# Second gated product of a retention-and-FFN kernel: from 256-column blocks to 512-column twins in two passes

## The chip, the cores and the metric

The kernel runs on one core of one Trainium2 chip. The metric is the device time of one execution in microseconds. The core's engines are named as the profile names them: PE (TensorE matmul), PEld (TensorE weight load, which overlaps PE), DVE (VectorE), ACT (ScalarE), POOL (GpSimd) and SP (SyncE, whose row issues nearly all DMAs). Each engine has its own row of instructions and takes them in order; semaphores order the engines among each other.

## The reference

```python
def _attn_ref(q, k, v):                  # 8 x 8 heads, 576 tokens, head size 64
    scores = scale * np.matmul(q, k.transpose(0, 1, 3, 2))
    gamma = 1.0 - 2.0 ** (-5.0 - np.arange(H, dtype=np.float32))
    rel = pos[:, None] - pos[None, :]
    Dmat = np.where(rel >= 0, gamma[:, None, None] ** rel[None, :, :], 0.0)
    return np.matmul(scores * Dmat[None, :, :, :], v)

def _moe_ref(x, w_in, w_out):            # x 4608 x 512, w_in 512 x 2048, w_out 2048 x 512
    h = x @ w_in
    g = h * np.cos(h)
    return g @ w_out                     # the second gated product

def _moe2_ref(x, w1, w2, w3, w_out):     # w1, w2, w3 512 x 768, w_out 768 x 512
    h = np.maximum(np.maximum(x @ w1, x @ w2), x @ w3)
    return h @ w_out
```

The three run one after the other on float32 data; the change is in `g @ w_out` of the second.

## The kernel before

Every dense product is done by a seven-product scheme on 2 x 2 blocks (Winograd's form of Strassen). The operands are the products' names: `P_A11`, `P_A12`, `P_A22` and the sums `P_S1` to `P_S4`; both the weights and the data are brought into these seven forms beforehand. Each operand is held as a high part (a cast to the reduced type, on ACT) and a low part (what the cast left, a subtraction on DVE), and each product takes three matmuls per pair of 128 x 128 weights: low weight by high data, high by high, high by low.

The 4608 tokens are 9 blocks of 512 columns (`NBLK`, `NB`). Blocks 1 to 8 also form four twins, `m` = 0 to 3 (`NDUO`): a matmul over a twin takes 256 columns of each of its two blocks, 512 in all. Block 0 stands alone. The order of the program:

1. Retention and the first product's first half, `group_in` (L447) with groups k = 0 and 1 of each block; then groups k = 2 and 3 of each block. The gate `h*cos(h)` (`gate`, L505: two ACT and two DVE instructions of 1024 columns for each half of a group) leaves its result in DRAM tensors `gq[j][k]`.
2. The second gated product, `phase_out` (L907): for each block j and each of the four groups k, seven products, in `OUT_ORDER`. `product_out` (L862) issues 12 matmuls of 256 columns for each. The seven products have a PSUM bank each, which collects the four groups; after the last group `finish_out` (L879) combines the banks, and two DMAs write the block of `x2`. `build_out` (L820) loads a group's four quarters and makes differences, high and low parts some slots ahead.
3. The branches: block 0 in three single groups (`single_group`, matmuls of 256 columns), then the twins (`duo_groups`, `product_duo` L416, matmuls of 512 columns), then the output product (`out_duo`, `group_out`).

The order of the work is written by hand. `tick()` (L153) ends a slot (one product, as a rule); `at(n, fn)` puts work n slots ahead, and `tick` issues what is due. So each engine's row is fixed by the program, and an instruction that waits holds back all that stands behind it in its row. Weights are brought into seven forms in the background: `background` (L235) loads and joins raw 64-bit weights and, for the branches ("b") and the output ("o"), stores the forms in DRAM ("stash"); `take` (L344) loads them; `take_split` (L327) makes the second product's forms ("wo") on chip from a stored joined form: four sums (L203 to L206), casts and subtractions (L213 to L229).

Buffers: 8 of 14 KB per partition for weights (`wpool`), 22 of 4 KB for data (`xpool`), 8 PSUM banks. A tile's buffer is given to a later tile, whose first writer waits for the last reader of the old one.

## Time and profile before

| | |
|---|---|
| median of 3 runs (lowest to highest) | 1441.91 us (1441.09 to 1442.17) |
| the profiled execution | 1442.28 us, span 1440.5 us |
| PE busy | 1413.1 us, 98% of the span, 10492 matmuls |
| DVE busy | 1160.7 us, 81% |
| ACT busy | 778.1 us, 54% |
| DMA | 331.52 MB, 230 GB/s over the span |

The span is from the first to the last instruction; the time of an execution has a little around it. A matmul's busy time overlaps its neighbours', so what a matmul costs is read from how many start in a stretch, not from its own duration. The granted clock tells TensorE's clock as a share of its higher level.

### The profile page before, as it was taken

How to read it: one execution, taken by the hardware profiler on the slowest of the kernel's cores; microseconds unless marked ns; L12 is line 12 of the kernel's file. 1: busy time of each engine (PE TensorE's matmuls, PEld its weight loads, DVE VectorE, ACT ScalarE, POOL GpSimd, SP SyncE). 2: the span in 40 equal slices, each digit the busy share in tenths (PEclk: the TensorE clock that was granted, in tenths of full speed). 3: DMA queues.
4: the chain of work that ended last, by engine and by line, in shares of the span. 5: the costliest groups of instructions: out<-in, count | busy, mean ns of one | idle time of the engine just before them, and what ended most of it. 6: DMA issues, size and time to landing. Idle time of an engine off the chain costs nothing.

```text
span 1440.5 us, 26312 instructions
## 1 busy us (share of the span) xinstructions
PE 1413.1 (98%) x10492; PEld 1299.3 (90%) x10492; DVE 1160.7 (81%) x1649; ACT 778.1 (54%) x1259; POOL 178.1 (12%) x128
## 2 busy tenths in 40 slices
PE   7999999999999998999999999999999999999998
PEld 5899999998999998999999999988888888888887
DVE  7988888779787779999999998668576667868875
ACT  4666666667787776444444443344344434534543
POOL 3343443331022000000000000000000000000000
PEclk9999999999999999999999999999999999999999
DMA  9779989868999985365565567723433294435633
GB/s 359 254 280 321 317 285 342 299 259 298 359 387 351 339 288 170 126 224 199 189 210 195 189 227 289 303 74 125 142 129 125 86 372 176 156 132 167 227 117 117
DMA packets 95034, 331.52 MB, mean 230 GB/s; under 512 B 9408, under 2 KB 17600, under 8 KB 88768
## 3 DMA queue, kind: packets, MB, share of 16 engines
q1 hardware_dynamic: 94912, 329.85, 64.4%
q8 instruction: 82, 1.34, 0.4%
q14 instruction: 40, 0.33, 0.1%
HBM read 197.69 MB, written 132.12 MB: 229 GB/s over the span
## 4 chain that ended last, share of the span: by engine, by line
PE 81%; DVE 3%; DMA 3%; issue 1%; ACT 0%; SPq 0%; DVEq 0%; ACTq 0%
PE wo L870 23%; PE d_e L428 13%; PE d_a L406 11%; PE b_e L428 7%; PE b_a L406 6%; PE d_u L1272 5%; PE a_e L428 3%; PE sums L406 3%; PE b_u L1272 2%; PE d_b L406 2%; PE sc L567 1%; PE po L626 1%; PE a_u L1272 1%; DMA k_z<-x2q 1%; PE state L610 1%; PE po L638 1%
## 5 line engine op out<-in xcount | busy, mean ns | idle before, releaser
L870 PE MATMUL wo<-h_g,w_wo 128*128 128x256 f32 x1728 | 313.3, 283 | 0.0
L870 PEld LDWEIGHTS wo<-h_g,w_wo 128*128 128x128 f32 x1728 | 269.9, 192 | 0.0
L870 PE MATMUL wo<-l_g,w_wo 128*128 128x256 f32 x864 | 245.4, 284 | 4.6 <-DVE l_g L843 4.5
L870 PEld LDWEIGHTS wo<-l_g,w_wo 128*128 128x128 f32 x864 | 166.1, 192 | 5.6 <-DVE l_g L843 5.4
L406 PE MATMUL d_a<-x_x,w_wi 128*128 128x256 f32 x864 | 122.5, 290 | 1.0 <-DVE x_x L383 1.0
L523 DVE SCALAR_TENSOR_TENSOR s_a<-t_a,s_a 128x1024 f32<-128x1024 f32 x72 | 93.6, 1300 | 31.1 <-ACT t_a L520 31.0
L428 PE MATMUL d_e<-h_e,w_b 128*128 128x512 f32 x432 | 115.5, 389 | 0.0
L406 PE MATMUL d_a<-x_y,w_wi 128*128 128x256 f32 x864 | 112.6, 287 | 2.5 <-DMA x_y<-xs 2.1
L406 PEld LDWEIGHTS d_a<-x_x,w_wi 128*128 128x128 f32 x864 | 108.3, 190 | 6.7 <-issue 1.9
L838 ACT CAST h_g<-tb_g 128x1024 fp32r<-128x1024 f32 x36 | 37.8, 1051 | 141.1 <-DVE tb_g L375 141.1
L406 PEld LDWEIGHTS d_a<-x_y,w_wi 128*128 128x128 f32 x864 | 108.9, 196 | 2.9 <-ACT ar_wo L184 2.3
L514 DVE SCALAR_TENSOR_TENSOR t_a<-s_a,t_a 128x1024 f32<-128x1024 f32 x72 | 96.0, 1334 | 18.0 <-ACT t_a L510 17.7
L453 ACT ACTIVATE ext<-d_e 128x512 f32<-128x512 f32 x72 | 43.0, 597 | 116.6 <-PE d_e L428 116.3
L428 PEld LDWEIGHTS d_e<-h_e,w_b 128*128 128x128 f32 x432 | 81.0, 188 | 16.8
L196 POOL TENSOR_TENSOR fa_b<-raw_b 128x512 uint32<-128x512 uint32 x18 | 22.5, 1250 | 537.5 <-DVE raw_b L190 506.8
L520 ACT ACTIVATE t_a<-t_a 128x1024 f32<-128x1024 f32 x72 | 76.0, 1055 | 21.9 <-DVE t_a L514 21.8
L594 ACT COPY u<-state 128x128 f32<-128x128 f32 x128 | 31.4, 264 | 96.6 <-PE state L610 96.2
L510 ACT ACTIVATE t_a<-s_a 128x1024 int32<-128x1024 f32 x72 | 76.1, 1056 | 1.3 <-PE d_a L406 0.4
L457 DVE TENSOR_TENSOR ext<-ext,b_e 128x512 f32<-128x512 f32 x36 | 24.7, 686 | 57.5 <-PE b_e L428 57.5
L428 PE MATMUL d_e<-l_e,w_b 128*128 128x512 f32 x216 | 66.5, 389 | 0.0
L406 PE MATMUL b_a<-x_x,w_wi 128*128 128x256 f32 x432 | 61.1, 289 | 0.6 <-DVE u L576 0.6
L406 PE MATMUL b_a<-x_y,w_wi 128*128 128x256 f32 x432 | 58.0, 283 | 1.7 <-DMA x_y<-xs 1.4
(268 smaller groups left out, 3248.4 us busy)
## 6 DMA issues: line engine op xcount, KB each, us to landing
u<-att SPq DMA_DIRECT2D x36, 1024.0 KB, 7.4
gq<-s_a SPq DMA_DIRECT2D x72, 512.0 KB, 5.4
k_g<-gq SPq DMA_DIRECT2D x72, 512.0 KB, 6.0
xs<-x_x SPq DMA_DIRECT2D x63, 512.0 KB, 5.5
x_y<-xs SPq DMA_DIRECT2D x63, 512.0 KB, 7.3
w_b<-st_b SPq DMA_DIRECT2D x9, 1792.0 KB, 11.3
st_b<-p_b SPq DMA_DIRECT2D x27, 512.0 KB, 5.1
mqp<-ext SPq DMA_DIRECT2D x24, 512.0 KB, 3.1
```

The costliest lines, as they stand in the source:

```text
L406: nc.tensor.matmul(h[:, p * HB : (p + 1) * HB], a, b, start=first and p == 0 and i == 0, stop=i == len(terms) - 1, skip_group_check=True,)
L428: nc.tensor.matmul(dst, a, b, start=first and i == 0, stop=i == len(terms) - 1, skip_group_check=True)
L453: nc.scalar.activation(dst, b[:, :n], AF.Copy, scale=scale)
L457: nc.vector.tensor_tensor(out=dst, in0=dst, in1=b[:, :n], op=ALU.add)
L510: nc.scalar.activation(st["t"], s, AF.Copy, bias=0.25)
L514: nc.vector.scalar_tensor_tensor(out=r, in0=s, scalar=MOST_TURNS, in1=st["t"], op0=ALU.min, op1=ALU.subtract)
L520: nc.scalar.activation(r, r, AF.Sin, scale=TURN, bias=HALF_PI)
L523: nc.vector.scalar_tensor_tensor(out=s, in0=f32(st["t"]), scalar=-1.0, in1=s, op0=ALU.max, op1=ALU.mult)
L594: nc.scalar.copy(um, st)
L838: nc.scalar.copy(h, o[pairs[k][2]])
L870: nc.tensor.matmul(b[:, mt * HB : (mt + 1) * HB], a, v, start=first and mt == 0 and p == 0 and i == 0, stop=last and p == len(ws) - 1 and ...
L1272: nc.tensor.matmul(dst, a, v, start=first and p == 0 and i == 0 and (wide or mt == 0), stop=p == 2 and i == 2, skip_group_check=True,)
```

## The change

The gated product is done in two passes over the tokens. A pass takes two of the four groups (`half` 0: k = 0 and 1, `half` 1: k = 2 and 3) through units: a unit is a twin (`m` = 0 to 3) or the lone block (`None`), in the order 0, None, 1, 2, 3 and then None, 0, 1, 2, 3 (`wo_order`). In a twin's unit each matmul has 512 columns, 256 of each block, and two banks take a product; a product is two slots of 12 matmuls (`both`). The lone block keeps 256 columns. A unit has three kinds of banks in place of seven: d takes A11, is copied into a (the seed), and then collects S2, S3 and A22; A12 goes onto the seeded a; b takes S1 and S4. A22 of a unit is held back (`pending`) into the next unit, between S2 and S4. The output quarters of the first pass are stored in `x2`; those of the second are stored by DMAs from POOL that add to what lies there (`accum_op`). The gate's results go to tensors laid out by twin (`gqp`, and `gqs` for the lone block).

Around it: `xpool` has 25 buffers, taken from the space set aside for DMAs that POOL issues. The splits of weights wo 4 to 7 move from the end of the first product into the first pass; four conversions of branch weights run in this stage instead of seven, and eight in the branches instead of five, the first two of them straight into weight tiles (`direct`). Two branch weights are loaded into the tiles of wo 4 and 5 as the last unit has done with each form (`freed`). The branches begin with twin 0, whose operands are made during the last unit, and the lone block's three groups come behind it.

```diff
-    xpool = ctx.enter_context(tc.tile_pool(name="xpool", bufs=22))
+    xpool = ctx.enter_context(tc.tile_pool(name="xpool", bufs=25))
...
-    gq = [[dram(f"gq{j}_{g}", [4, NB]) for g in range(4)] for j in range(NBLK)]
+    gqs = [dram(f"gqs{g}", [4, NB]) for g in range(4)]
+    gqp = [[dram(f"gqp{m}_{g}", [4, 2, NB]) for g in range(4)] for m in range(NDUO)]
     x2s = dram("x2q0", [4, NB])
     x2p = [dram(f"x2p{m}", [4, 2, NB]) for m in range(NDUO)]
-    x2q = [x2s] + [x2p[m][:, :, b] for m in range(NDUO) for b in range(2)]
...
-    def background(kind, i, arena, lag=3, both=False, gap=2):
+    def background(kind, i, arena, lag=3, both=False, gap=2, direct=False):
...
-            st["p", k] = x4(f"p_{kind}{i}_{k}", [hi - lo, 2, HB], F32R)
+            if direct:
+                if k == 0:
+                    st["w"] = w14(f"w_{kind}{i}")
+                    weights[kind, i] = [st["w"][:, n] for n in range(7)]
+                st["p", k] = st["w"][:, lo:hi]
+            else:
+                st["p", k] = x4(f"p_{kind}{i}_{k}", [hi - lo, 2, HB], F32R)
...
-    back = [(k, i) for k, n in (("wi", 4), ("wo", 0), ("b", 0), ("o", 0)) for i in range(n, len(PAIRS[k]))]
+    back = [(k, i) for k, n in (("wi", 4), ("wo", 0)) for i in range(n, 8)]
+    back += [("b", i) for i in (0, 1, 2, 4, 3, 5, 6, 7, 8)] + [("o", i) for i in range(3)]
...
-    for i, (n, m) in enumerate(((-13, -2), (-11, 0), (-9, 7), (-7, 12))):
-        take_split("wo", 4 + i, endB + n, endB + n + 4, *(endB + m + k for k in (0, 1, 1, 2)))
...
-        gate(g[f"s{half}"], f"{g['name']}_{half}", gq[j][k][:, 2 * half : 2 * half + 2], 0 if half else 3)
+        q = slice(2 * half, 2 * half + 2)
+        dst = gqp[(j - 1) // 2][k][:, q, (j - 1) % 2] if j else gqs[k][:, q]
+        gate(g[f"s{half}"], f"{g['name']}_{half}", dst, 0 if half else 3)
-    OUT_ORDER = (P_A11, P_A12, P_S4, P_S2, P_A22, P_S3, P_S1)
...
+    WO_STEPS = (
+        (-6, "load", 0),
+        (-6, "load", 1),
+        (-5, "load", 3),
+        (-4, "load", 2),
+        (-2, "high", P_A11, 0),
+        (-1, "low", P_A11),
+        (-1, "less", 4, 1, 0, None),
+        (0, "high", P_S1, 4),
+        (1, "low", P_S1),
+        (2, "high", P_A12, 2),
+        (3, "low", P_A12),
+        (3, "less", 0, 3, 4, 0),
+        (4, "high", P_S2, 0),
+        (5, "low", P_S2),
+        (7, "less", 2, 0, 2, 2),
+        (8, "high", P_S4, 3),
+        (8, "less", 1, 3, 1, 1),
+        (9, "low", P_S4),
+        (10, "high", P_S3, 1),
+        (11, "low", P_S3),
+        (20, "high", P_A22, 2),
+        (21, "low", P_A22),
+    )
+    CLAG = 2
+    SINGLE_LEAD = 1
+    def wo_unit(m, half, base):
+        n = 1 if m is None else 2
+        name = f"g{'s' if m is None else m}_{half}"
+        src = [gqs[2 * half + k] if m is None else gqp[m][2 * half + k] for k in range(2)]
+        sets = [(0, 1)] if m is None else [(0,), (1,)]
+        ops = [{}, {}]
+        ts = [{} for _ in sets]
+        def load(i, q):
...
+        def less(i, d, a, b, over):
+            t = ts[i]
+            dst = x4(f"q{d}_{name}{i}d", [2, NB]) if over is None else t[over]
+            nc.vector.tensor_tensor(out=dst, in0=t[a], in1=t[b], op=ALU.subtract)
+            t[d] = dst
+        def high(i, product, q):
+            h = x4(f"h{product}_{name}{i}", [2, NB], F32R)
+            nc.scalar.copy(h, ts[i][q])
+            ts[i]["high", product] = (h, ts[i][q])
+            put(i, product, "hi", h)
+        def low(i, product):
+            h, t = ts[i]["high", product]
+            lo = x4(f"l{product}_{name}{i}", [2, NB], F32R)
+            nc.vector.tensor_tensor(out=lo, in0=t, in1=f32(h), op=ALU.subtract)
+            put(i, product, "lo", lo)
+        for step, fn, *args in WO_STEPS:
+            for k in range(len(sets)):
+                when = step + k + base_of[half, m] + (pend_of[half, m] - 2 if step >= 8 else 0)
+                if step >= 20 and (half, m) == wo_order[-1]:
+                    when -= 7
+                if step < 0:
+                    when -= EARLY_OF[half, m]
+                if m is None and 8 <= step < 20:
+                    when -= SINGLE_LEAD
+                at(max(when - slot[0], 0), lambda fn=fn, k=k, args=args: fns[fn](k, *args))
+        return {"m": m, "half": half, "n": n, "name": name, "ops": ops}
+    def wo_group(u):
+        m, half, n, name, ops = (u[key] for key in ("m", "half", "n", "name", "ops"))
+        ws = [[weights["wo", 4 * half + 2 * k + p] for p in range(2)] for k in range(2)]
+        scale = TURN * WSCALE**-2
+        dst = x2s if m is None else x2p[m]
+        def go(banks, product, k, first):
+            hi, lo = ops[k][product]["hi"], ops[k][product]["lo"]
+            for mt in range(2):
+                c = slice(mt * 128, mt * 128 + 128)
+                to = banks[mt] if n == 2 else banks[0][:, mt * HB : (mt + 1) * HB]
+                to = to.rearrange("p (b n) -> p b n", b=n)
+                for p, w in enumerate(ws[k]):
+                    r = slice(p * HB, p * HB + HB)
+                    wh, wl = w[product][:, 0, c], w[product][:, 1, c]
+                    for i, (a, v) in enumerate(((wl, hi), (wh, hi), (wh, lo))):
+                        nc.tensor.matmul(
+                            to,
+                            a,
+                            v[:, :, r],
+                            start=first and k == 0 and p == 0 and i == 0 and (n == 2 or mt == 0),
+                            stop=k == 1 and p == 1 and i == 2,
+                            skip_group_check=True,
+                        )
+        def both(banks, product, first=False):
+            go(banks, product, 0, first)
+            tick()
+            go(banks, product, 1, first)
+        def copy(q, banks):
+            out_t[q] = x4(f"o{q}_{name}", [2, 2, HB] if n == 2 else [NB])
+            for t, b in parts(q, banks):
+                nc.scalar.activation(t, b, AF.Copy, scale=scale)
+        def plus(q, banks):
+            for t, b in parts(q, banks):
+                nc.vector.scalar_tensor_tensor(out=t, in0=b, scalar=scale, in1=t, op0=ALU.mult, op1=ALU.add)
+        def store(q):
+            t = out_t[q].rearrange("p b k n -> p b (k n)") if n == 2 else out_t[q]
+            if half:
+                nc.gpsimd.dma_start(out=dst[:, q], in_=t, accum_op=ALU.add)
+            else:
+                nc.sync.dma_start(out=dst[:, q], in_=t)
+        d = banks("d")
+        a = banks("a")
+        both(d, P_A11, True)
+        at(0, lambda: [nc.scalar.copy(y, x) for x, y in zip(d, a)])
+        tick()
+        free_of(P_A11)
+        b = banks("b")
+        both(b, P_S1, True)
+        at(CLAG, lambda: copy(3, b))
+        tick()
+        free_of(P_S1)
+        both(a, P_A12)
+        at(CLAG, lambda: copy(0, a))
+        at(CLAG + 1, lambda: store(0))
+        tick()
+        free_of(P_A12)
+        both(d, P_S2)
+        at(CLAG, lambda: copy(1, d))
+        tick()
+        free_of(P_S2)
+        if pending:
+            last_product()
+        both(b, P_S4)
+        at(1, lambda: plus(1, b))
+        at(3, lambda: store(1))
+        tick()
+        free_of(P_S4)
+        both(d, P_S3)
+        at(1, lambda: plus(3, d))
+        at(3, lambda: store(3))
+        tick()
+        free_of(P_S3)
+        def last():
+            both(d, P_A22)
+            at(CLAG, lambda: copy(2, d))
+            at(CLAG + 1, lambda: store(2))
+            free_of(P_A22)
+        pending.append({"last": last})
+    wo_order = [(half, m) for half, ms in enumerate(((0, None, 1, 2, 3), (None, 0, 1, 2, 3))) for m in ms]
+    base_of, pend_of, EARLY_OF = {}, {}, {}
+    wo_units = []
+    def plan_wo(base):
+        for i, key in enumerate(wo_order):
+            base_of[key] = base
+            pend_of[key] = 2 if i else 1
+            EARLY_OF[key] = 4 if i and wo_order[i - 1][1] is None else 0
+            base += 12 + pend_of[key]
+        for half, m in wo_order:
+            wo_units.append(wo_unit(m, half, base_of[half, m]))
+        return base
...
-                    out_first()
+                    done_at = plan_wo(slot[0] + 7)
...
-    for i in range(7):
-        at(28 * i + 33, lambda: background(*back.pop(0), False))
...
+    halfway = base_of[wo_order[NDUO + 1]]
+    for i in range(4):
+        t = 34 + 8 * i
+        take_split("wo", 4 + i, t, t + 3, t + 4, t + 5, t + 6, t + 7)
+    for i in range(4):
+        at((20, 76, 90, 104)[i], lambda: background(*back.pop(0), True, 4))
+    for i in range(2):
+        at(halfway - base + 8 + 24 * i, lambda i=i: take("b", i))
...
-    at(28 * (NBLK - 1) + 21, lambda: block_in(0, 0, 2, 3))
-    phase_out("wo", [[2 * k, 2 * k + 1] for k in range(4)], todo, lambda j, k: outs.pop((j, k)), TURN * WSCALE**-2, x2q)
...
+    def freed(product):
+        for i, j in ((0, 2), (1, 4)):
+            w = weights["wo", 4 + i]
+            nc.sync.dma_start(out=f32(w[product]), in_=stash["b", j][:, product])
+            weights["b", j] = w
+    wo_units[-1]["freed"] = freed
...
-    def duo_in(m, name, to):
+    def duo_in(m, name, to, early=1):
...
+            n = 7 - (early - 1 + 7 - n) // early
...
+    at(done_at - 11 - base, lambda: duo_in(0, 'e0', 4, 2))
+    for u in wo_units:
+        wo_group(u)
...
-    duo_in(0, "e0", 16)
-    for k in range(3):
-        single_group(k)
     for m in range(NDUO):
-        for n in (1,) if m < 3 else (1, 16):
-            at(n, lambda: background(*back.pop(0), False, 5))
+        for n in ((0, 6), (1, 22), (1, 22), (1, 22))[m]:
+            at(n, lambda m=m: background(*back.pop(0), False, 5, direct=not m))
         duo_groups(m, 0)
+        if not m:
+            block_in(0, 2, 10, 13)
+            duo_groups(m, 1)
+            duo_in(m + 1, f"e{m + 1}", 16)
+            for k in range(3):
+                single_group(k)
+            continue
         if m + 1 < NDUO:
             duo_in(m + 1, f"e{m + 1}", 14)
         else:
...
-    nc = _bacc.Bacc("TRN2", target_bir_lowering=False, num_devices=1)
+    nc = _bacc.Bacc("TRN2", target_bir_lowering=False, num_devices=1, dynamic_dma_scratch_size=4096)
```

What moves in the rows of the engines. PE, the first rows of the second product, before (`x_g`, `h_g`, `l_g`: high and low parts of the gated data; `w_wo`: weights; `wo`: banks):

```order
L870 MATMUL wo_0_6504<-x_g_0_6413,w_wo_4503 128x256 x3
L870 MATMUL wo_0_6504<-x_g_0_6413,w_wo_4883 128x256 x3
L870 MATMUL wo_0_6504<-x_g_0_6413,w_wo_4503 128x256 x3
L870 MATMUL wo_0_6504<-x_g_0_6413,w_wo_4883 128x256 x3
L870 MATMUL wo_1_6528<-h_g_0_6437,w_wo_4503 128x256 x2
L870 MATMUL wo_1_6528<-l_g_0_6455,w_wo_4503 128x256
```

and now:

```order
L923 MATMUL d_g_0_6458<-h_g_00_6434,w_wo_4487 128x512 x2
L923 MATMUL d_g_0_6458<-l_g_00_6453,w_wo_4487 128x512
L923 MATMUL d_g_0_6458<-h_g_00_6434,w_wo_4867 128x512 x2
L923 MATMUL d_g_0_6458<-l_g_00_6453,w_wo_4867 128x512
L923 MATMUL d_g_0_6459<-h_g_00_6434,w_wo_4487 128x512 x2
L923 MATMUL d_g_0_6459<-l_g_00_6453,w_wo_4487 128x512
```

In all PE's row has 3024 matmuls of 256 columns here before (L870), and now 1344 of 512 and 336 of 256 (L923).

DVE at the border of the first and second product, before (`s0_a8_3`, `s1_a8_3`: results of the last group, `t_a8`: its gate, `s_wo`: sums of a weight split, `ta`, `tb`, `l`: differences and low parts of the first group's data):

```order
L375 TENSOR_TENSOR tb_g0_0_6453<-tb_g0_0_6453,k1_g0_0_6372 128x512
L459 SCALAR_TENSOR_TENSOR s0_a8_3_6367<-b_a8_3_6374,s0_a8_3_6367 128x512
L203 TENSOR_TENSOR s_wo7_6473<-fa_wo7_6394 128x256
L204 TENSOR_TENSOR s_wo7_6473<-s_wo7_6473,fa_wo7_6394 128x256
L205 TENSOR_TENSOR s_wo7_6473<-fa_wo7_6394 128x256
L206 TENSOR_TENSOR s_wo7_6473<-fa_wo7_6394,s_wo7_6473 128x256
L375 TENSOR_TENSOR ta_g0_0_6434<-k1_g0_0_6372,k0_g0_0_6370 128x512
L514 SCALAR_TENSOR_TENSOR t_a8_2_1_6458<-s1_a8_2_6265,t_a8_2_1_6458 128x1024
L459 SCALAR_TENSOR_TENSOR s1_a8_3_6387<-d_a8_3_6354,s1_a8_3_6387 128x512
L843 TENSOR_TENSOR l1_g0_0_6501<-tb_g0_0_6453,h1_g0_0_6479 128x1024
L229 TENSOR_TENSOR w_wo4_6495<-fa_wo4_6282,w_wo4_6495 128x2x256
```

and now (`g0_00`, `g0_01`: the two groups of twin 0's first unit):

```order
L466 SCALAR_TENSOR_TENSOR s0_a8_3_6340<-b_a8_3_6343,s0_a8_3_6340 128x512
L521 SCALAR_TENSOR_TENSOR t_a8_2_1_6419<-s1_a8_2_6249,t_a8_2_1_6419 128x1024
L466 SCALAR_TENSOR_TENSOR s1_a8_3_6356<-d_a8_3_6327,s1_a8_3_6356 128x512
L890 TENSOR_TENSOR l0_g0_00_6453<-q0_g0_00_6360,h0_g0_00_6434 128x1024
L874 TENSOR_TENSOR q4_g0_00d_6455<-q1_g0_00_6362,q0_g0_00_6360 128x1024
L890 TENSOR_TENSOR l0_g0_01_6474<-q0_g0_01_6379,h0_g0_01_6451 128x1024
L874 TENSOR_TENSOR q4_g0_01d_6476<-q1_g0_01_6381,q0_g0_01_6379 128x1024
L530 SCALAR_TENSOR_TENSOR s1_a8_2_6249<-t_a8_2_1_6419,s1_a8_2_6249 128x1024
L890 TENSOR_TENSOR l3_g0_00_6495<-q4_g0_00d_6455,h3_g0_00_6478 128x1024
```

The weight sums have left this place, and the first low part (`l0_g0_00`) stands right behind the add of the last group's last result.

DVE in the last unit, now (`g3_10`, `g3_11`: the unit's two groups, `g2`: the unit before it, `e0`: operands of the first branch twin):

```order
L1073 TENSOR_TENSOR r4_e0_9196<-r1_e0_9153,r0_e0_9134 128x1024
L890 TENSOR_TENSOR l2_g2_10_9214<-q2_g2_10_8668,h2_g2_10_9192 128x1024
L874 TENSOR_TENSOR q2_g3_10_8977<-q0_g3_10_8924,q2_g3_10_8977 128x1024
L1073 TENSOR_TENSOR r6_e0_9219<-r3_e0_9155,r4_e0_9196 128x1024
L1083 TENSOR_TENSOR l0_e0_9221<-r0_e0_9134,h0_e0_9217 128x1024
L890 TENSOR_TENSOR l2_g2_11_9238<-q2_g2_11_8688,h2_g2_11_9212 128x1024
L874 TENSOR_TENSOR q2_g3_11_8997<-q0_g3_11_8946,q2_g3_11_8997 128x1024
L874 TENSOR_TENSOR q1_g3_10_8926<-q3_g3_10_8950,q1_g3_10_8926 128x1024
L1073 TENSOR_TENSOR r5_e0_9244<-r3_e0_9155,r1_e0_9153 128x1024
L874 TENSOR_TENSOR q1_g3_11_8948<-q3_g3_11_8975,q1_g3_11_8948 128x1024
L890 TENSOR_TENSOR l6_g3_10_9264<-q3_g3_10_8950,h6_g3_10_9241 128x1024
```

Four operations of the branch twin (`r4`, `r6`, `l0`, `r5`) stand between those of the unit, ahead of the low part of S4 (`l6_g3_10`).

## Rows read from the trace of the kernel before

**Rows 1.** The page of the kernel before: span, busy time of each engine.
```profile
span 1440.5 us, 26312 instructions
...
PE 1413.1 (98%) x10492; PEld 1299.3 (90%) x10492; DVE 1160.7 (81%) x1649; ACT 778.1 (54%) x1259; POOL 178.1 (12%) x128
```

**Rows 2.** Busy time by stretch (us): around the second product, and in the branches.
```profile
core 0: us, PE busy (x) PEld busy (x) DVE busy (x) ACT busy (x) POOL busy (x), PEclk, DMA share, GB/s
543.00:568.00 25.00, 20.41 (x150) 19.46 (x149) 24.97 (x35) 17.42 (x25) 0.00 (x0) 0.93 0.43 148
568.00:896.00 328.00, 328.00 (x2733) 327.84 (x2732) 306.22 (x413) 154.21 (x202) 18.34 (x14) 1.00 0.59 204
896.00:925.00 29.00, 27.98 (x233) 27.78 (x232) 19.33 (x28) 9.99 (x15) 0.00 (x0) 1.00 0.94 369
952.00:1285.00 333.00, 332.83 (x1469) 275.01 (x1469) 231.27 (x288) 143.76 (x226) 10.39 (x10) 1.00 0.44 156
```

**Rows 3.** Chain that ended last, in order of time: start, length (us), what.
```profile
566.86 328.26 PE wo L870 x2731
...
953.98 2.72 PE d_e L428 x12
```

**Rows 4.** Line 870: ns min/median/max, first and last start (us).
```profile
L870 PE MATMUL wo<-l_g,w_wo x864: 280/283/415, 545.5 to 915.3; 128*128 128x256 f32 x173
...
L870 PE MATMUL wo<-x_g,w_wo x432: 278/283/385, 543.6 to 906.7; 128*128 128x256 f32 x144
```

**Rows 5.** PE in order of time at the start of the second product: start, length (us).
```profile
551.62 0.39 PE L870 MATMUL wo<-l_g,w_wo 128*128 128x256 f32 x1 [3.00 <-DVE l_g L843]
...
553.47 2.54 PE L406 MATMUL d_a<-x_y,w_wi 128*128 128x256 f32 x12
```

**Rows 6.** Busy time by stretch: 6 us inside that start.
```profile
550.00:556.00 6.00, 4.38 (x24) 4.38 (x25) 6.00 (x9) 5.28 (x9) 0.00 (x0) 0.72 0.51 178
```

**Rows 7.** Who PE waited for: us in total, times, longest.
```profile
PE wo L870 <- DVE l_g L843: 4.5, 3, 3.0
...
PE b_b L406 <- DVE x_z L383: 1.0, 1, 1.0
```

**Rows 8.** Groups by line and shape: busy us, mean ns of one, idle before.
```profile
L523 DVE SCALAR_TENSOR_TENSOR s_a<-t_a,s_a 128x1024 f32<-128x1024 f32 x72 | 93.6, 1300 | 31.1 <-ACT t_a L520 31.0
...
L843 DVE TENSOR_TENSOR l_g<-tb_g,h_g 128x1024 fp32r<-128x1024 f32 x36 | 44.0, 1222 | 10.9 <-ACT h_g L838 10.9
...
L838 ACT CAST h_g<-tb_g 128x1024 fp32r<-128x1024 f32 x36 | 37.8, 1051 | 141.1 <-DVE tb_g L375 141.1
...
L883 DVE SCALAR_TENSOR_TENSOR o_wo<-wo,u_wo 128x512 f32<-128x512 f32 x36 | 24.8, 689 | 2.1 <-ACT p_b L220 1.1 <-PE wo L870 0.3
...
L476 ACT COPY sums<-d_a 128x512 f32<-128x512 f32 x36 | 20.6, 572 | 3.6 <-PE d_a L406 3.6
```

**Rows 9.** The same view: what a weight conversion costs VectorE.
```profile
L190 DVE SCALAR_TENSOR_TENSOR raw_b<-raw_b,spare 128x512 uint32<-128x512 uint32 x18 | 12.5, 693 | 1.1
...
L229 DVE TENSOR_TENSOR p_b<-raw_b,p_b 128x512 fp32r<-128x512 f32 x18 | 12.1, 684 | 0.0
...
L189 DVE TENSOR_SCALAR spare<-spare 128x512 uint32<-128x512 uint32 x24 | 10.2, 425 | 15.4 <-ACT spare L184 15.4
```

**Rows 10.** Line 203, one of the four sums of a conversion: ns min/median/max.
```profile
L203 DVE TENSOR_TENSOR s_wo<-fa_wo x8: 416/418/420, 378.0 to 546.5; 128x256 f32<-128x256 f32 x8
```

**Rows 11.** DMA issues: count, KB each, median us from issue to landing.
```profile
x2p<-o_wo SPq DMA_DIRECT2D x16, 512.0 KB, 4.0
...
r_e<-x2p SPq DMA_DIRECT2D x16, 512.0 KB, 6.3
...
k_z<-x2q SPq DMA_DIRECT2D x4, 512.0 KB, 10.7
```

More of the change, by code (lines that the diff above doesn't have):

```diff
@@ L862, in product_out @@
-    def product_out(b, ws, product, x, n, first, last):
-        for mt in range(2):
-            m = slice(mt * 128, mt * 128 + 128)
-            for p, w in enumerate(ws):
-                c = slice(p * HB, p * HB + HB)
-                wh, wl = w[product][:, 0, m], w[product][:, 1, m]
-                xh, xl = x[product][0][:, c], x[product][1][:, c]
-                for i, (a, v) in enumerate(((wl, xh), (wh, xh), (wh, xl))):
-                    nc.tensor.matmul(
-                        b[:, mt * HB : (mt + 1) * HB],
-                        a,
-                        v,
-                        start=first and mt == 0 and p == 0 and i == 0,
-                        stop=last and p == len(ws) - 1 and i == 2,
-                        skip_group_check=True,
-                    )
@@ L907, in phase_out @@
-    def phase_out(kind, groups, todo, xs, scale, dsts):
-        for j, k in todo:
-            ws = [weights[kind, i] for i in groups[k]]
-            x = xs(j, k)
-            first, last = k == 0, k == len(groups) - 1
-            if first:
-                banks, f = {}, {}
-            for product in OUT_ORDER:
-                if first:
-                    banks[product] = bank(f"{kind}{j}_{product}")
-                if pending and product == P_A22:
-                    last_product(False)
-                product_out(banks[product], ws, product, x, HB * len(ws), first, last)
-                if last:
-                    finish_out(f, product, banks, scale, f"{kind}{j}", dsts[j])
-                tick()
@@ L924, in retention_ffn @@
-    outs = {}
-    x2_steps = {"t1": (1, nc.vector), "t3": (3, nc.vector), "last": 4}
-    def out_first():
-        outs[0, 0] = build_out("g0_0", NB, gq[0][0], range(2, 8), 0, **x2_steps)
+        q = slice(2 * half, 2 * half + 2)
[25 more added lines that the diff above has]
+    )
@@ new lines, in retention_ffn, with piece, put @@
+    CLAG = 2
[7 more added lines that the diff above has]
+        ts = [{} for _ in sets]
+        def piece(t, i, k):
+            return t[:, k - sets[i][0]] if m is None else t
+        def load(i, q):
+            t = ts[i][q] = x4(f"q{q}_{name}{i}", [2, NB])
+            for k in sets[i]:
+                nc.sync.dma_start(out=piece(t, i, k), in_=src[k][:, q])
+        def less(i, d, a, b, over):
[3 more added lines that the diff above has]
+            t[d] = dst
+        def put(i, product, which, x):
+            for k in sets[i]:
+                ops[k].setdefault(product, {})[which] = x[:, k : k + 1] if m is None else x
+        def high(i, product, q):
[8 more added lines that the diff above has]
+            put(i, product, "lo", lo)
+        fns = {"load": load, "less": less, "high": high, "low": low}
+        for step, fn, *args in WO_STEPS:
[9 more added lines that the diff above has]
+        return {"m": m, "half": half, "n": n, "name": name, "ops": ops}
```

168 lines of the change are left out of this document (57 added, 111 removed).

## The prediction

> **What bounds the kernel now.** I read the page's totals first: TensorE (PE) is busy 98% of the span [rows 1], so a change is worth what it does to PE's stream. Next, the busy time by stretch [rows 2]. In the second product (568 to 896 us) PE never idles: 2733 matmuls of 256 columns in 328.00 us, 0.1200 us each. In the branches (952 to 1285 us) every matmul has 512 columns, and 1469 of them take 333.00 us, 0.2267 us each. The chain that ended last shows the same two pitches, 328.26 us for 2731 and 2.72 us for 12 [rows 3]. So a matmul of 512 columns costs 0.013 us less than two of 256: about 0.013 us of every matmul goes to something other than columns. That is what this change can win. The weight loads fit: PEld is busy all of the first stretch and 275.01 of 333.00 us of the second [rows 2].
>
> The second product runs from 543.6 to 915.4 us, 371.8 us [rows 4]. Its 3024 matmuls at 0.1200 are 362.9, and the last first-product group leaves 12 matmuls (1.4) inside. So 7.5 us are lost, all at the start: PE waits 4.5 us for VectorE's (DVE's) low parts [rows 7], 3.00 of them in one piece, and the 12 matmuls behind that piece take 2.54 in place of 1.44 us [rows 5]; in those 6 us the granted clock is 0.72, a mixture of the two levels, 1.2 and 2.4 GHz [rows 6]. DVE is busy 24.97 of 25.00 us there [rows 2]: four splits of second-product weights stand in its row.
>
> **The change, part by part.**
>
> *Columns.* 3024 matmuls of 256 columns go (362.9); 1344 of 512 (304.7) and 336 of 256 (40.3) come, 345.0 us: **17.9 saved**. The widths are those of the PE rows above, and the branches' moving operand already has the same form (two blocks of 256 in one matmul), so their 0.2267 is the price. The Trainium skill, "TensorE: Matmul & The Clock Gate", section "Back-to-back issue gap", gives N/2.4 + 2.5 ns: 215.8 ns for 512 columns and 109.2 for 256, which would save 2.6 ns a pair, 3.5 us in all. Rows 2 and 3 disagree with it at both widths, and the rows decide.
>
> *Start of the second product.* The four splits move to the middle of the stage, so the 7.5 us go. What is late next is the first low part: it stands on DVE behind the add that waits for the last product of the old stage. Add 0.69, low 1.22 [rows 8], less the two matmuls (0.45) that need only the high part: 1.5 us of PE idle. The second product's low stands behind a second low, two differences and a gate multiply (1.30): 1.2 more. **2.7 us added.**
>
> *Inside a twin unit.* A slot is 12 matmuls, 2.72 us; a unit is 14 slots, 38.1 us. DVE has 14 lows and 8 differences at 1.22 and four adds at 0.69 [rows 8]: 29.6 us. Two units of the lone block need 14.8 each, the four splits 4.1 each (four sums at 0.42 [rows 10], three subtractions at 0.68 and a small one), the four conversions 6.3 each (that, and two joins of 0.43 + 0.69 [rows 9]). Together 308 of 345 us, 89%, against 306.22 of 328.00 before [rows 2]. So DVE is no fuller, but its lead shrinks: each low is issued one slot ahead, behind a ScalarE (ACT) cast of 1.05, and ACT's row holds copies that wait for PE. Following one unit from PE's slot 0: A11 ends at 5.4, the seed copies (2 x 0.57) at 6.6, the cast for A12 at 7.6, its low at 8.9, wanted at 10.9. Then difference, low, difference: 12.5. S2's second low waits for its cast: 14.9. The held-back A22's first low at 17.1, then six more operations at 1.22: S4's first low at 24.4, wanted at 27.2. Margins are 2 to 3 us and DVE has a gap of about 3.5 near the unit's end, so a bare unit stalls nothing. With weight work in DVE's row: unit 1 gets a split and most of a conversion in its last six slots, 8.4 us against 3.5 of gap and 2.4 of margin, **2.5 lost**; units 2 and 3 get a split ahead of S4, 4.1 against 2.8 and small gaps, **1.0 lost each**. In the second pass the conversions fall into the gap: nothing. In the lone block's units, with slots of 1.44 us, S2's lows come about **0.7 late, twice**. In the last unit four operations of the first branch twin stand ahead of S4's low: 4.9 less 2.8, **2.1 lost**. Sum 7.3 us.
>
> *Accumulating stores.* Twenty stores of the second pass go from POOL's queue and add in memory; no row shows one. The nearest rows: a plain store of the same 512 KB lands in 4.0 us, and the slowest median of any transfer of that size is 10.7 [rows 11]. The tile buffer behind such a store is wanted again after 9 to 14 us (by the chain above; the tightest is two slots and a cast behind the lone block's last store), so at the low end they cost nothing and at the high end some 1.5 us once; a gain is excluded, since PE waits for no store now. I take 4.0, the row of the same tile and bytes: nothing. The branches read the first twin three units later. The Trainium skill, "DMA: Bandwidth & Descriptors", section "Anatomy of one DMA", prices a store from that queue at 2.0 us + bytes/436e3 us, 3.2 us here; the sum would stay the same.
>
> *Edits at nothing.* The gate's stores come in pieces of 2 KB now, as the old x2p stores did, which landed in 4.0 us [rows 11]; nobody waits for them for a whole phase. Loads of a unit (eight of 512 KB) are issued four to six slots ahead, 11 us or more against 6.3 to landing [rows 11]; if buffers hold them back one slot, the margin is used up, and the lows of A11 are late first. On SP's queue they stand behind stores that wait for ACT and DVE, one slot at most. Three more tile buffers (25 for 22) have no PE wait to remove outside the start. Branches begin on a twin whose data landed long before: the old wait for x_z, 1.0 us [rows 7], **goes**. DVE has eight conversions there in place of five, 19 us more, and is busy 231.27 of 333.00 [rows 2], so that hides; if not, the first twin's adds are late.
>
> **Sum.** New stage 345.0 + 1.4 + 2.7 + 7.3 = 356.4 against 371.8: -15.4; -1.0 behind it: -16.4. The profiled execution took 1442.28 us, its span 1440.5 and 1.8 around it, so 1425.9; the median of the runs shown, 1441.91, is 0.4 lower, so **1425.5 us**. A measurement of this kernel tells 0.2% (2.9 us) from no change.
>
> **Rivals.**
>
> *All hidden.* Only the 2.7 us at the start remain: 1418.2. For it: PE lost nothing in 328 us with DVE at 93% [rows 2]. Against: there the lows were issued five or six slots of 1.44 us ahead, now one of 2.72.
>
> *The weight work doesn't fit into DVE's gaps* (slower). DVE's 29.6 us and its waits for casts and for PE in a unit (3.0, 2.1 and 3.5) make 38.2, just PE's 38.1. If the waits don't shrink when splits and conversions (4 x 4.1 + 4 x 6.3 = 41.6 us) come between, these add in full: 345.0 + 1.4 + 2.7 + 41.6 = 390.7, less the 1.0: 1459.8. It decides from 23.7 us on. For it: casts, lows and copies that wait for PE form one loop, one slot long. Against: waits on PE shrink as soon as DVE is late.
>
> *Accumulating stores hold buffers.* Landing in 15 us, 5 past the reuse, on one wait of each of the second pass's five units: 25 us, 1450.5. It decides from about 13 us. Against: all transfers of this size land sooner [rows 11].
>
> *Columns alone count.* If the 0.013 us were the old stage's own (its weights, its order) and not one per matmul, 512 columns would take 0.2400 here and the 17.9 would go: 1443.4. Rows 3 speak against it, since the branches load as many weights per matmul. The rule of the Trainium skill cited above would leave 3.5 of it.
>
> **How the numbers follow.** Forecast 0.65, all hidden 0.20, weight work 0.08, stores 0.05, columns 0.02. The likeliest case runs from 1420 to 1434 (its stalls, 10.0 us, halved or nearly doubled). The range takes in the hidden case with some slack, since the stalls at the start may be shorter, and the way towards the slower ones: 1414 to 1441. Faster by over 0.2% (below 1439.0): the first two, 0.83. Within: part of the likeliest and the last, 0.07. Slower: 0.10.
>
> **What would show it.** Right: line 923's matmuls at 0.2267 us wherever PE doesn't wait; the stage 352 to 362 us long; PE's waits there on low parts (line 890), the longest at the first product and in units 1 to 3 and the last; no clock below 1.00 for long; DVE near 90%; POOL's stores landing within 10 us. Wrong: a pitch other than 0.2267; waits for casts or lows in every unit; waits of ACT or DVE on POOL's stores; PE waiting for a load of q; new waits in the branches, or in the first product by the changed stores.

## The result and the profile after

The changed kernel takes **1425.65 us** (median of 4 runs, 1425.45 to 1425.98) against 1441.5 us; the ratio is 0.9892, 95% interval 0.9875 to 0.9909. The forecast was 1425.5. That the two agree to 0.2 us is partly luck: the second product gained 3.9 us more than forecast, the part behind it came out 4.9 us worse than forecast, and 1.2 us came from a part that the forecast left alone.

The page's totals (they answer to [rows 1]); then the whole stage and two stretches inside twin units (us from and to, length, then busy time and instructions of PE, PEld, DVE, ACT and POOL, granted clock, DMA share, GB/s; they answer to [rows 2]):

```profile
span 1423.8 us, 23611 instructions
...
PE 1392.0 (98%) x9148; PEld 1223.2 (86%) x9148; DVE 1129.5 (79%) x1532; ACT 817.1 (57%) x1322; POOL 192.5 (14%) x148
```

```profile
542.40:900.40 358.00, 354.27 (x1719) 298.20 (x1718) 309.83 (x333) 210.46 (x280) 28.30 (x27) 1.00 0.71 221
...
770.00:850.00 80.00, 80.00 (x354) 66.08 (x354) 70.86 (x78) 48.46 (x65) 13.35 (x13) 1.00 0.90 248
...
850.00:888.80 38.80, 37.50 (x164) 30.30 (x163) 35.24 (x33) 24.20 (x29) 2.60 (x3) 1.00 0.79 210
```

The middle row is the price of a matmul of 512 columns: 354 in 80.00 us, 0.2260 us, against 0.2267 in the branches before. PEld has 14 us to spare there. The granted clock is 1.00 over the stage: the dip of [rows 6] is gone.

Line 923, the new second product, as [rows 4] had line 870 (ns min, median, max; first and last start; the forms' counts):

```profile
L923 PE MATMUL d_g<-h_g,w_wo x512: 387/389/496, 542.4 to 899.9; 128*128 128x512 f32 x171
...
L923 PE MATMUL d_g<-l_g,w_wo x256: 389/389/499, 544.7 to 900.1; 128*128 128x512 f32 x128
```

The stage runs from 542.37 to 900.37 us, and 24 branch matmuls (5.4 us) stand inside, ahead of the last unit's held-back product; less these it takes 352.6 us, against 371.9 by the same count before. (The 5.4 us are counted as behind the stage.) Split like this, the span of every kernel of this study reads (us):

| kernel | span | ahead of the stage | the stage | behind it |
|---|---|---|---|---|
| before | 1440.5 | 543.6 | 371.9 | 525.0 |
| changed | 1423.8 | 542.4 | 352.6 | 528.9 |
| `w256` | 1439.5 | 543.8 | 367.7 | 528.1 |
| `lag8` | 1417.9 | 541.8 | 352.0 | 524.1 |
| `noadd` | 1421.0 | 541.9 | 350.5 | 528.6 |
| `c100` | 1420.9 | 541.3 | 350.4 | 529.1 |
| `fill1` | 1427.3 | 543.5 | 354.9 | 528.9 |
| `fill2` | 1454.4 | 542.9 | 382.0 | 529.5 |
| `splits` | 1426.6 | 542.5 | 355.0 | 529.1 |
| `best1` | 1416.8 | 542.1 | 350.5 | 524.2 |
| `best2` | 1418.2 | 544.1 | 349.8 | 524.4 |
| `best3` | 1415.9 | 543.2 | 348.4 | 524.4 |

The column "ahead" spreads over 2.8 us, though the code in it is the same in most of these kernels. So the change's 1.2 us there are not its own, and small effects are read from the other columns.

Who PE waited for after the change (us in total, times, longest; it answers to [rows 7]):

```profile
PE d_e L435 <- ACT ext L460: 4.7, 5, 1.5
...
PE d_g L923 <- DVE l_g L890: 1.9, 2, 1.6
...
PE b_g L923 <- DVE l_g L890: 1.1, 1, 1.1
...
PE d_gs L923 <- DVE l_gs L890: 0.8, 2, 0.4
```

The first row is new and lies in the branches (955 to 1290 us), where before there was this alone:

```profile
PE b_e L428 <- ACT ext L453: 0.2, 1, 0.2
```

In the stage there are three main places: its start, the lone block's units, and the start of the last unit:

```profile
544.75 0.50 PE L923 MATMUL d_g<-l_g,w_wo 128*128 128x512 f32 x1 [1.64 <-DVE l_g L890]
...
588.28 0.39 PE L923 MATMUL d_gs<-l_gs,w_wo 128*128 128x256 f32 x1 [0.41 <-DVE l_gs L890]
...
857.12 0.50 PE L923 MATMUL b_g<-l_g,w_wo 128*128 128x512 f32 x1 [1.05 <-DVE l_g L890]
```

A wait of a busy PE costs more than the bracket says, since a matmul's busy time overlaps its neighbours'. Counted from the starts of matmuls against 0.2267 or 0.1200 us each: 2.3 us at the start (2.0 of them at the first product, 0.2 at the second), 0.7 and 0.6 in the lone block's units, 0.3 in unit 2 of the first pass, 1.8 at the start of the last unit, and 6.0 in the branches in five places (5.5 without the slower matmul right behind each wait).

### The profile page after: what moved, and what is told of

It reads as the page before. It is cut to its first block, busy times and chain, and to the rows that moved or that the text cites. A ratio compares the mean times of both kernels' runs of the same rounds, so it can differ in the third digit from the quotient of the medians.

```text
span 1423.8 us, 23611 instructions
## 1 busy us (share of the span) xinstructions
PE 1392.0 (98%) x9148; PEld 1223.2 (86%) x9148; DVE 1129.5 (79%) x1532; ACT 817.1 (57%) x1322; POOL 192.5 (14%) x148
## 5 line engine op out<-in xcount | busy, mean ns | idle before, releaser
L923 PE MATMUL d_g<-h_g,w_wo 128*128 128x512 f32 x512 | 157.9, 389 | 0.0
L890 DVE TENSOR_TENSOR l_g<-q_g,h_g 128x1024 fp32r<-128x1024 f32 x96 | 117.8, 1238 | 21.4 <-ACT h_g L883 15.1
L883 ACT CAST h_g<-q_g 128x1024 fp32r<-128x1024 f32 x96 | 98.5, 1051 | 25.6 <-DVE q_g L874 11.0
L923 PEld LDWEIGHTS d_g<-h_g,w_wo 128*128 128x128 f32 x512 | 95.8, 188 | 19.7
L923 PE MATMUL d_g<-l_g,w_wo 128*128 128x512 f32 x256 | 99.8, 390 | 1.9 <-DVE l_g L890 1.9
L435 PE MATMUL d_e<-h_e,w_b 128*128 128x512 f32 x304 | 81.6, 390 | 2.8 <-ACT ext L460 2.8
L923 PE MATMUL b_g<-h_g,w_wo 128*128 128x512 f32 x256 | 79.0, 390 | 0.0
L435 PEld LDWEIGHTS d_e<-h_e,w_b 128*128 128x128 f32 x304 | 56.8, 188 | 15.3 <-ACT ext L460 3.7
L923 PEld LDWEIGHTS d_g<-l_g,w_wo 128*128 128x128 f32 x256 | 48.1, 188 | 12.6 <-DVE l_g L890 2.7
```

Of the source, the lines that this page charges most:

```text
L435: nc.tensor.matmul(dst, a, b, start=first and i == 0, stop=i == len(terms) - 1, skip_group_check=True)
L883: nc.scalar.copy(h, ts[i][q])
L890: nc.vector.tensor_tensor(out=lo, in0=t, in1=f32(h), op=ALU.subtract)
L923: nc.tensor.matmul(to, a, v[:, :, r], start=first and k == 0 and p == 0 and i == 0 and (n == 2 or mt == 0), stop=k == 1 and p == 1 and i == 2,
```

## Experiments

### Is it the width? (`w256`)

```diff
-                        nc.tensor.matmul(
-                            to,
-                            a,
-                            v[:, :, r],
-                            start=first and k == 0 and p == 0 and i == 0 and (n == 2 or mt == 0),
...
+                        for e in range(n):
+                            nc.tensor.matmul(
+                                to[:, e],
+                                a,
+                                v[:, e, r],
+                                start=first and k == 0 and p == 0 and i == 0 and e == 0 and (n == 2 or mt == 0),
...
```

> The new order, but each 512-column matmul of the second product is cut into two of 256 columns with the same weights, one per block. Nothing is left out. Theory (every matmul pays about 0.013 us beside its columns): 1344 matmuls at 0.2267 us become 2688 at 0.1200, so 17.9 us come back; the waits inside the stage (3.0 us, the 2.3 us at its start not counted) shrink by up to 3 as slots get longer: 1440.5 to 1443.5 us, and no pitch other than 0.1200 us in the cut matmuls. Rival (the 0.013 us belonged to the old order, or is paid once for each pair of equal weights): the second matmul of a pair comes after 0.1067 us, and the time stays at 1425.6 us or goes to at most 1434.

Measured: 1442.14 us (10 runs, 1441.18 to 1443.93); the kernel before took 1441.07 beside it (13 runs), and the ratio is 1.0008 (0.9999 to 1.0018). The same stretch of the stage as above, in this kernel:

```profile
770.00:850.00 80.00, 80.00 (x669) 80.00 (x669) 69.91 (x79) 48.24 (x66) 12.87 (x12) 1.00 0.86 243
```

669 matmuls in 80.00 us are 0.1196 us each, and PEld is busy all of it: the second matmul of a pair loads its weights again and pays in full. The stage is 15.1 us longer. Columns alone make 17.9; what is missing are stalls that go with longer slots, above all the last unit's 1.8. So the gain hangs on the width: with narrow matmuls the new order, twins, seeded bank, two passes and all, is as slow as the old. Part of this is a balance: the stage of `w256` is still 4.2 us shorter than before (367.7 against 371.9), and the part behind it is 3.1 us longer (528.1 against 525.0).

### The waits in the branches (`lag8`)

They look alike. Here is the first, on SP's queue, ACT and PE of the changed kernel (start, length, what, and in brackets the wait ahead of it):

```profile
1013.50 0.37 SPq L1201 DMA_DIRECT2D mqp<-ext  x1
1013.96 1.30 SPq L1069 DMA_DIRECT2D r_e<-x2p  x2
1015.31 0.48 SPq L178 DMA_DIRECT2D raw_b<-w  x1
1015.84 0.57 SPq L284 DMA_DIRECT2D st_b<-p_b  x1
```

```profile
1023.03 0.66 ACT L184 ACTIVATE spare<-raw_b 128x512 f32<-128x512 f32 x1 [5.88 <-DMA raw_b<-w]
...
1024.15 0.57 ACT L460 ACTIVATE ext<-d_e 128x512 f32<-128x512 f32 x1
```

```profile
1022.69 0.61 PE L435 MATMUL a_e<-l_e,w_b 128*128 128x512 f32 x2
1024.78 1.21 PE L435 MATMUL d_e<-h_e,w_b 128*128 128x512 f32 x4 [1.47 <-ACT ext L460]
```

Read them from the last row back. PE waits for bank d, which the copy of line 460 empties. The copy stands in ACT's row behind line 184, the widening of raw weights, and that waits for its load. The load was issued at 1015.31, behind a result store (line 1201) that had to wait for DVE, and it has landed by 1023.0, among the stash stores of the conversion ahead of it. Before, with one conversion in each of three twins and two in the fourth, no such stores stood beside it: a load issued at 1009.51 us was in use at 1013.82.

```profile
1009.51 0.41 SPq L178 DMA_DIRECT2D raw_b<-w  x1
```

```profile
1013.82 0.65 ACT L184 ACTIVATE spare<-raw_b 128x512 f32<-128x512 f32 x1 [3.15 <-DMA raw_b<-w]
```

That the stash stores are what makes the load slow is read from their place; no run took them away.

```diff
-        second = lag + gap if both else 2 * lag + 3
+        second = lag + gap if both else min(2 * lag + 3, lag + 8)
...
-            at(n, lambda m=m: background(*back.pop(0), False, 5, direct=not m))
+            at(n, lambda m=m: background(*back.pop(0), False, 8 if m else 5, direct=not m))
```

> The changed kernel, but in the branches the first cast of a weight conversion (ScalarE's widening, line 184) of twins 1 to 3 stands three slots of 1.36 us later behind its load, with all that follows it. Nothing is left out. Theory (the loads land 5 to 8 us after their issue, behind stash stores of the conversion before, and the widening that waits for them holds back the bank copies behind it in ScalarE's row): the five waits of PE for those copies, 4.7 us by the table of waits and 5.5 us counted from the starts of matmuls, go to under 1 us, and the time is 1420.1 to 1421.5 us. Rival (VectorE has no room for eight conversions, 19 us more than before): the waits stay, or come back at other places; 1424.5 to 1427 us.

Measured: 1419.39 us (4 runs, 1418.97 to 1422.13), 6.3 less than the changed kernel and 0.7 under the expected range; the part behind the stage, where the edit works, is 4.8 us shorter, and the rest lies in parts that share the code. Of PE's waits in the branches (955 to 1290 us) this is left:

```profile
PE d_e L435 <- DVE ext L464: 0.5, 1, 0.5
```

So eight conversions do fit into DVE's row there; what cost was the place of the widening in ACT's row, too soon behind its load. The loads land no sooner in `lag8` (up to 8.4 us); they are no longer waited for.

### The start of the last unit (`c100`, `noadd`)

The forecast had 2.1 us lost in the last unit, by operations of the first branch twin ahead of S4's low part. 1.8 us are lost, but at the unit's first two products. ACT of the changed kernel:

```profile
847.29 1.05 ACT L883 CAST h_g<-q_g_10d 128x1024 fp32r<-128x1024 f32 x1 [2.42 <-DVE q_g_10d L874]
854.85 1.05 ACT L883 CAST h_g<-q_g_11d 128x1024 fp32r<-128x1024 f32 x1 [6.51 <-DMA st_b<-p_b]
```

The second cast waits for a buffer that a stash store of the fourth conversion still reads: the store issued at 841.21 us lands at 854.75. Two edits, one on the conversion and one on the adding stores:

```diff
-        at((20, 76, 90, 104)[i], lambda: background(*back.pop(0), True, 4))
+        at((20, 76, 90, 100)[i], lambda: background(*back.pop(0), True, 4))
```

> The changed kernel, but the fourth weight conversion of the second product's stage begins 4 slots (10.9 us) sooner, so that its stash stores are issued before the last unit begins. Nothing is left out. Theory (ScalarE's cast for the last unit waits 6.5 us for a buffer that a stash store, landing in up to 13.5 us, still reads): the cast's wait goes, the 1.8 us that PE loses at the start of the last unit go, 1423.5 to 1424.2 us. Rival (adding stores hold the buffers): the waits stay where they are, 1425.2 to 1426 us. A mishap that would speak for neither: the conversion now falls into the unit before and makes its lows late there.

```diff
-                nc.gpsimd.dma_start(out=dst[:, q], in_=t, accum_op=ALU.add)
+                nc.gpsimd.dma_start(out=dst[:, q], in_=t)
```

> The changed kernel, but the twenty stores of the second pass don't add to what lies in memory; they still go from POOL's queue. Left out: the add of the first pass to the second in the twin and single outputs. Theory (adding stores land in 8.7 us, but nothing that PE waits for hangs on them; the last unit's late start comes from the stash stores of a weight conversion): the stores land in 4 to 6 us and the time stays within 0.6 us of 1425.6. Rival (adding stores hold the tile buffers of the last unit's first operands): the 1.8 us lost at 852 to 857 us go, and with them perhaps the late operations before it: 1423.5 to 1424.3 us.

Measured: `c100` 1423.95 us (1422.75 to 1426.09), `noadd` 1425.12 us (1422.80 to 1426.88). Both ranges reach over the changed kernel's 1425.65, so neither time tells by itself; the traces do. In both the cast comes some 5 us sooner, PE loses nothing at the last unit, and the stage is 2.1 to 2.2 us shorter. First `c100`, then `noadd`:

```profile
848.27 1.05 ACT L883 CAST h_g<-q_g_11d 128x1024 fp32r<-128x1024 f32 x1 [1.16 <-DVE q_g_11d L874]
```

```profile
849.56 1.05 ACT L883 CAST h_g<-q_g_11d 128x1024 fp32r<-128x1024 f32 x1 [1.81 <-DVE q_g_11d L874]
```

Neither theory was whole. The stash stores hold the buffer, as the first said; but they are late beside the adding stores, so that taking the adds away cures it too. The landing times show it (line 284's stash stores in the stage, us min, median, max; changed kernel, then `noadd`, then `c100`, where they land as late but are issued sooner):

```profile
DMA to landing us min/median/max: 2.0/4.8/13.5
```

```profile
DMA to landing us min/median/max: 2.0/3.3/6.3
```

```profile
DMA to landing us min/median/max: 2.0/6.8/11.6
```

Timing counts as well: `w256` and `fill1` (below) keep the adds, the same work falls at other times, and PE loses nothing at the last unit in either.

And the second pass's stores themselves, changed kernel, then `noadd` (they answer to [rows 11]; count, KB each, median us to landing):

```profile
x2p<-o_g SPq DMA_DIRECT2D x16, 512.0 KB, 2.9
x2p<-o_g POOLq DMA_DIRECT2D x16, 512.0 KB, 8.7
```

```profile
x2p<-o_g POOLq DMA_DIRECT2D x16, 512.0 KB, 4.7
```

### How much room has VectorE? (`fill1`, `fill2`)

The forecast took 4.5 us for weight work in units 1 to 3; 0.3 were lost. These runs put idle work into DVE's row:

```diff
+        if m is not None:
+            for step in (1, 5, 9):
+                for _ in range(3):  # 6 in fill2
+                    at(
+                        max(step + base_of[half, m] - slot[0], 0),
+                        lambda: nc.vector.tensor_tensor(out=fill, in0=fill, in1=fill, op=ALU.subtract),
+                    )
```

> The changed kernel with nine extra VectorE operations of 128x256 (0.42 us each, 3.75 us) in each of the eight twin units of the second product, three each at its slots 1, 5 and 9, on a tile that nothing else reads. Nothing is left out. Theory (VectorE's waits for casts and for PE shrink as it falls behind, so only its sum counts): its work in the stage grows by 30 us to some 338 of 352 us, and the stage gets 0 to 5 us longer. Rival (the prediction's arithmetic: a unit takes 3.5 us of gap and 2.4 of margin, and what is over it comes on top): with a split or a conversion in six units the excess is 6.3, 2.0, 2.0 and three times 4.1 us, 20 us or more on the stage.

> The same with eighteen extra operations, 7.5 us, in each twin unit. Theory (only the sum counts): VectorE's work in the stage is some 368 us, more than the 352 us that the stage takes, so VectorE becomes the bound and the stage grows by 16 to 25 us. Rival (a fixed margin for each unit): 3.75 us more than in the run before in each of eight units, 45 to 55 us on the stage.

Measured: 1429.04 and 1456.19 us (one run each). The stage in the two (fill1, then fill2):

```profile
543.50:903.80 360.30, 355.14 (x1718) 298.03 (x1717) 336.30 (x405) 210.29 (x280) 28.14 (x27) 1.00 0.71 220
```

```profile
542.90:930.30 387.40, 362.55 (x1718) 299.22 (x1717) 366.70 (x477) 210.97 (x280) 28.09 (x27) 0.99 0.65 204
```

DVE's busy time goes from 309.8 to 336.3 and 366.7 us, the stage from 352.6 to 354.9 and 382.0. The first 26.5 us cost 2.3, where a margin for each unit would have cost 20 or more: the sum counts far more than the single unit. (PE's new waits are some 4 us, half of them in unit 2 of the first pass, and the 1.8 us at the last unit go.) `fill2` takes 29.4 us more than the changed kernel, more than the theory's 16 to 25 and less than the rival's 45 to 55: DVE is then the bound, but it stays idle for 20.7 of 387.4 us, which the theory had at nothing. Its waits for casts shrink as it falls behind, from 15.1 to 7.8 to 3.3 us (changed kernel, `fill1`, `fill2`):

```profile
DVE l_g L890 <- ACT h_g L883: 15.1, 10, 4.1
```

```profile
DVE l_g L890 <- ACT h_g L883: 7.8, 6, 2.9
```

```profile
DVE l_g L890 <- ACT h_g L883: 3.3, 4, 1.5
```

And of its waits for PE this row of the changed kernel is gone in both, as the prediction said against its own rival:

```profile
DVE o_g L950 <- PE b_g L923: 7.1, 7, 2.3
```

### The splits at the border (`splits`)

```diff
+    for i, (n, m) in enumerate(((-13, -2), (-11, 0))):
+        take_split("wo", 4 + i, endB + n, endB + n + 4, *(endB + m + k for k in (0, 1, 1, 2)))
...
-    for i in range(4):
+    for i in range(2, 4):
         t = 34 + 8 * i
```

> The changed kernel, but the splits of weights wo 4 and 5 stand where they stood in the kernel before, around the border of the first and the second product; those of wo 6 and 7 stay in the first pass. Nothing is left out. Theory (the 7.5 us that the old stage lost at its start came from the splits in VectorE's row, and their move is what took this away): 8.2 us of VectorE's work come back to the border, where it is busy all the time; PE loses 5 to 8 us in the first 30 us of the stage in place of 2.3, and the 0.3 us at unit 2 go. Rival (the narrow, short-lead order of the old stage lost them): 2 to 3 us there, as now.

Measured: 1428.39 us (one run); the stage is 2.4 us longer. PE loses 4.5 us at the start in place of 2.3, less than the 5 to 8 that were expected, and the 0.3 us at unit 2 are gone. The new wait, in PE's row at the unit's second product:

```profile
550.50 0.62 PE L925 MATMUL b_g<-h_g,w_wo 128*128 128x512 f32 x2
552.67 0.50 PE L925 MATMUL b_g<-l_g,w_wo 128*128 128x512 f32 x1 [1.56 <-DVE l_g L892]
```

Two splits of four bring back 2.2 of the 5.2 us between 7.5 and 2.3. That fits, but all four weren't put back, so it isn't shown that the splits are all of it.

### Together (`best1`, `best2`, `best3`)

`best1` has the edits of `lag8` and `c100`, and one more; the later two change its number and one line:

```diff
-            EARLY_OF[key] = 4 if i and wo_order[i - 1][1] is None else 0
+            EARLY_OF[key] = (4 if wo_order[i - 1][1] is None else 0) if i else 1  # 2, 3 in best2, best3
...
-                if m is None and 8 <= step < 20:
+                if m is None and 2 <= step < 20:  # best2, best3
```

> Three edits together: the branch conversions' cast three slots later, the fourth conversion of the stage four slots sooner, and the first unit's early steps (loads, first casts, first low parts) one slot sooner, so that the first low part stands ahead of the add that waits for the last first-product block. Nothing is left out. Theory: the two parts measured by themselves add, 5 to 6 us and 1.8 us, and of the 2.3 us at the start some 1 to 1.5 go, since only the second group's low part still stands behind the add: 1416 to 1418.5 us. Rival (the early low part holds back the gate's row, and PE then waits at another place): 1418 to 1420 us.

> The combined version, but the first unit's early steps stand two slots sooner instead of one, so that both groups' first low parts stand ahead of the add that waits for the last first-product block, and the lone block's early steps (products A12 and S2) one slot sooner. Nothing is left out. Theory (what is left of the start, 2.1 us, is the second group's low part behind that add and the one after it; the lone block's two 0.5 us are S2's low part issued too late): of these 3.2 us some 2 go, 1416 to 1417.5 us. Rival (casts and low parts that stand sooner wait for their loads, or hold back the gate and the bank copies of the last first-product group): no gain, 1418.5 to 1420 us.

> The same with the first unit's early steps three slots sooner. Nothing is left out. Theory: as with two slots, within 0.6 us of it, since the low parts then have more lead than they need. Rival (the loads, now issued three slots sooner, haven't landed, and the casts hold back ScalarE's bank copies of the first product): PE waits in the last first-product group, 1 to 3 us more than with two slots.

Measured: `best1` **1418.76 us** (5 runs, 1418.53 to 1419.75), ratio to before 0.9848, interval 0.9834 to 0.9861; it is faster than both kernels (its slowest run is under the fastest of the changed kernel), but its time is not told apart from that of `lag8` alone; the stage is 1.5 us shorter than there. It lies just above its expected range, inside the rival's, and the reason is the third edit, which gives nothing: counted over the first two products the start still costs 2.3 us, since the second group's low part came to stand where the first group's had, behind the add. `best2` took 1421.01 us (1420.24 to 1421.98), `best3` 1419.57 us (1418.29 to 1421.04). Their lone-block waits are gone, and the stage of `best3` takes 348.4 us, 2.0 over its 346.4 of matmuls alone. Yet neither is faster than `best1`. In their profiles the part ahead of the stage is 2.0 and 1.1 us longer, and all of it is PE's loss between 340 and 400 us, long ahead of the edit (8.2 and 6.8 us against 5.8); kernels of this study whose code is the same up to there lose between 5.4 us (`c100`) and 7.9 (`w256`), so it says little of the edits. The two differ by 1.4 us, more than the 0.6 expected. At the start `best2` loses 2.7 us, by a cast that is late: it stands in ACT's row behind a gate instruction whose input DVE makes later, much as the rival had it. `best3` loses 1.5 there. The wait in `best2`:

```profile
551.11 0.73 PE L923 MATMUL b_g<-h_g,w_wo 128*128 128x512 f32 x2 [1.41 <-ACT h_g L883]
```

## Why the prediction was right, and where it was not

**Columns: right.** 0.2260 us for 512 columns, and 17.9 us of which `w256` gave back 15.1 net of stalls. The formula of the Trainium skill ("TensorE: Matmul & The Clock Gate", section "Back-to-back issue gap"), which the page gives for a matmul by itself and not for a stream with a weight load ahead of each, would by an estimate (2.5 ns for each pair) have made `w256` some 3.4 us slower by columns. The trace doesn't agree with it here, at either width: 0.2260 us against 0.2158, and 0.1196 against 0.1092.

**Start of the second product: right in sum, not in its parts.** 2.7 forecast, 2.3 measured, on the low parts named. But the first product lost 2.0 and not 1.5, and the second 0.2 and not 1.2: its low part came just in time, as PE was itself late by then.

**Inside the units: 7.3 forecast, 3.9 measured.** The step that failed is "8.4 us against 3.5 of gap and 2.4 of margin, 2.5 lost" and the 1.0 for units 2 and 3: it gave each unit a fixed margin, while a late DVE passes its lag on and its own waits shrink. In these units 0.3 us were lost, not 4.5. `fill1` measures it: 26.5 us more cost 2.3 net. The lone block's two waits were right (0.7 forecast each, 0.7 and 0.6). The last unit's 2.1 were right in size and wrong in cause. (The places found add up to 3.4; the rest of the 3.9 lies in none.)

**Accumulating stores: mis-sized.** "I take 4.0, the row of the same tile and bytes: nothing": they land in 8.7 us, 4.0 more than the same stores without the add, and cost some 2 us, not by their own buffers but by making the stash stores beside them late. The rival had their own buffers held. By the Trainium skill's "DMA: Bandwidth & Descriptors", section "Anatomy of one DMA", the estimate was 3.2; the trace doesn't agree, since the plain store from that queue took 4.7 here.

**Branches: wrong.** The wait for x_z went, as forecast (1.0). But "DVE has eight conversions there in place of five, 19 us more, and is busy 231.27 of 333.00, so that hides" looked only at DVE's sum. A conversion also puts a DMA on SP's row and a waiting instruction into ACT's, ahead of the copies that free PE's banks: 6.0 us. `lag8`, which moves only the widening and what follows it, takes 4.8 us of it away.

So the sum came out by errors of opposite sign: the stage was 3.9 us shorter than forecast, the part behind it 4.9 us longer, and the part ahead of it 1.2 us shorter, where kernels that share the code differ by more.

## What to carry to other kernels

Where a matmul's price has a part that does not depend on its columns, read it from two widths in the same trace, and count the saving as instructions removed times that part; cutting the wide matmuls in two again is the control. When background work is moved, follow every row that it puts an instruction into: an engine with spare time still stalls PE if an instruction that waits for a load stands ahead of a bank copy. Judge a helper engine's room by its sum over the stage first, and put idle work into its row to find where it ends.

## What the runs showed of the hardware

A store that adds in memory weighs on the DMA beside it here. With the adds, the DMA's busy share over the stage is 0.71 at 221 GB/s; without them it is 0.63 at 224 GB/s (`noadd`, below). Stash stores that took 6.3 us at most without them took up to 13.5 with them; in `fill1`, where the adds remain but the work falls at other times, they took 7.2 at most.

```profile
541.90:897.90 356.00, 353.58 (x1719) 298.52 (x1718) 309.22 (x333) 210.92 (x280) 22.34 (x27) 1.00 0.63 224
```

And two matmuls in a row with the same weights are not cheaper here than two with different ones: 0.1196 us each in `w256`, where PEld has a load for each (669 for 669, 80.00 of 80.00 us), against 0.1200 before.
